# One dense batch instead of two, and block batches turned by TensorE, in a BigBird attention and SwiGLU kernel

## The chip, the cores and the metric

The kernel runs on one core of a Trainium2 chip. Its time is the device time of one execution in microseconds; three executions took 307.23, 308.00 and 308.08 us, median 308.0 us. A profile of one execution (307.95 us) records when every engine was busy and every DMA transfer ran. The engines are TensorE (PE: matmuls, with weight loads counted apart as PEld), VectorE (DVE), ScalarE (ACT), GpSimd (POOL) and SyncE (SP, which only issues DMAs here). Each engine works through its own list of instructions in a fixed order; an instruction that has to wait holds up all that stand behind it in that list. DMAs are issued from the lists of SP, ACT and POOL.

## What is computed

Four batches, eight heads, 768 tokens, head width 64. Attention is block-sparse: the 768 tokens are 24 blocks of 32, and a query block sees its neighbours, the first and last block, and three sampled blocks; the first and last query block see everything. After it comes a SwiGLU feed-forward layer (FFN) on 3072 tokens of width 512, with 1536 hidden columns.

```python
scores = scale * np.matmul(q, k.transpose(0, 1, 3, 2))
mask = np.abs(blk_i - blk_j) <= 1
mask = mask | (blk_i == 0) | (blk_j == 0) | (blk_i == n_blocks - 1) | (blk_j == n_blocks - 1)
for qb in range(n_blocks):
    for kb in sampled_blocks[qb]:
        mask[qb*32:(qb+1)*32, kb*32:(kb+1)*32] = True
attn = softmax(np.where(mask, scores, -1e9)); o = np.matmul(attn, v)
x = o.transpose(0, 2, 1, 3).reshape(B * S, H * D)
xn = x / rms(x) * rms_g
out = (silu(xn @ w_gate) * (xn @ w_val)) @ w_out
```

Inputs and outputs are float32; `sampled_blocks` holds int64. The kernel multiplies in bfloat16.

## The kernel before

**Tiles and units.** The 3072 tokens are 24 tiles of 128. Tiles are put into units (`UNITS`): a unit's tiles go through the FFN together, so a projection matmul (`proj`, line 728) moves 128 columns for each tile of the unit. Batch 0 has units of 1, 1, 1 and 3 tiles, each of the batches 1 to 3 two units of 3, which makes ten units, 0 to 9. For a unit `u` and a group `f` of hidden columns the steps are `g` (gate projection, PE), `th` (tanh, ACT), `uu` (DVE), `v` (value projection, PE), `hp` (DVE); then `y` (output projection, PE, line 767), `yo` (scaling, ACT or DVE) and `so` (store, SP).

**Dense batches** (`NDB = 2`: batches 0 and 1). All 768 x 768 scores of each head are computed. The mask is not added: the keys carry 24 more rows that say which block a key is in, and the queries 24 rows with 0 or -32768 for each block, so that the matmul of 88 rows (`dk`, line 322) gives masked scores. `de` is the exponential (ACT, line 343), `av` the product with the values (`dav`, line 357), `xo` the division by the sum (DVE). Batch 0's keys and queries are turned (head dimension onto the partitions) by TensorE transposes (`tpx`, line 301), batch 1's by DMA transposes on SP's queue (`turn`, line 288).

**Block batches** (`NDB` to 3: batches 2 and 3). Keys, queries and values are loaded (lines 452 and 459, SP), converted into bfloat16 rows (`fill_k`, `fill_q`, `fill_v`: `sfk`, `sfq`, `sfv`), and keys and queries are turned by one DMA transpose each for a batch (`turn_k`, line 478; `turn_q`, line 504). The two token halves `c` of a pair of tokens lie apart in the turned keys. For a tile `n` of four query blocks the keys that it sees are gathered into `kg`: `kf` copies neighbours and the first and last block (`kg_fixed`; DVE or ACT), `kd` the sampled blocks, at addresses from registers (`kg_sampled`, POOL, line 146). The values go back to DRAM as bfloat16 rows (`st`, `store_v`, line 508) and are gathered from there: `pvi` (`pair_v`, lines 570 to 578, SP) fixed blocks, `gv` and `gw` (`block_v`, line 555) sampled ones, one DMA of 32 rows for each, two thirds on SP and one third on ACT. `qk` (line 599) are the scores of a tile, `exp` (line 605), `av` (line 648), `xo`. Tile 5 (`AT`) holds the first and last block, which see all keys (`qka`, line 615; `expa`, line 623).

**Block numbers.** DVE works out the row and column addresses of the sampled blocks (`table`), and they are loaded into registers of POOL (three loads), SP (three) and ACT (two) (`table_regs`, line 435), 16 or fewer at a time.

**Units into the FFN.** `sq`, `rsq`, `xq` normalise a unit's attention output; for units below `NPET = 6` it is turned by TensorE (`tr`, line 704) and evicted (`cp`); for the later ones by a DMA transpose on SP's queue (`xt`, line 715).

**Order.** The kernel is scheduled by a planner that runs when the program is built: `op(key, engines with a cost, what it depends on, priority, function, slots it takes, slots it gives back)` registers a step, and a loop picks, over all steps that are ready, the one that can start first (then by priority) and emits its instructions. So the lists of all engines follow from costs and priorities written in the code, and the chip keeps to these lists. Attention steps have better priorities (1 to 3) than projections (4, 5). PSUM is eight banks: scores take two at a time from 0 to 3 (`S_`), gate projections bank 4 (at some times also 6), value projections 5, output projections 6, attention output 7. Buffers have slots (`pools`): two for gathered keys, three for gathered values, three for raw loads.

Of the kernel before, what the change touches and what calls it, by code (L numbers as in the profile page):

```python
# [16 lines left out]
def kernel(  # L17
# [19 lines left out]
    P = 128  # L37
# [12 lines left out]
    NR, NHP, NXN, NYO, NPET = NRND, 2, 2, 3, 6  # L50
    NSLOT, NAUG, NOPEN, NDB = 5, 2, 2, 2
    IXAT, RGAT = 36.0, 48.0
    NPT, NPA, NKG, NVG, NRAW = 4, 2, 2, 3, 3
    AHEAD, HURRY, HURU = 0.8, ("av", "xo", "sq", "rsq", "xq", "tr", "cp"), 0
    NSTARV, ZPAT, NG2 = 3, 32.0, 4
    AH = {"uu": 0.3, "hp": 0.3}
    WARM = (11, 10, 2)
    HD = NC * D // 2
    UNITS = [(0, 0, 1), (0, 1, 1), (0, 2, 1), (0, 3, 3)]
    UNITS += [(b, c, 3) for b in range(1, NDB) for c in (0, 3)]  # L60
    ND = len(UNITS)
    for b in range(NDB, B):
        UNITS += [(b, (5, 0, 1), 3), (b, (2, 3, 4), 3)]
    NU = len(UNITS)
    HG = [("h", 0 if u < 3 else u) for u in range(NU)]
    HO = [u if u < 3 else 0 for u in range(NU)]
# [9 lines left out]
    def bank16(n):  # L76
# [12 lines left out]
    VAC = const.tile([P, 2, H * NC, D + 2], BF16, name="VAC")  # L89
    VGC = const.tile([P, 6, VW], BF16, name="VGC")  # L90
# [6 lines left out]
    RAWD = list(A)  # L97
    RAWS = [RAWC[:, i * RB:(i + 1) * RB] for i in range(NRAW)]
    aug = [AUG[:, i] for i in range(NAUG)]
    va_ = [VAC[:, i] for i in range(2)]  # L100
    vfl = [t.rearrange("p m d -> p (m d)")[:, 0:6 * VW] for t in va_]
    VAUG = [t.rearrange("p (t c h d) -> p t c h d", t=NC // 2, c=2, h=H) for t in (vfl[0], PTC[:, 10240:10240 + 6 * VW])]
    rt_ = RAWC[:, NRAW * RB:].bitcast(BF16)
    VGB = [VGC, rt_[:, 0:6 * VW].rearrange("p (x w) -> p x w", w=VW),
           vfl[1].rearrange("p (x w) -> p x w", w=VW)]
    PD = [PTC[:, i * PDW:(i + 1) * PDW] for i in range(3)]
    PTB = [t.rearrange("p (h l x) -> p h l x", h=2, l=2) for t in [rt_[:, 6 * VW:6 * VW + 1024]] + [
        PTC[:, i * 1024:(i + 1) * 1024] for i in range(NPT - 1)]]
    PAB = [PTC[:, 3072 + i * 2048:3072 + (i + 1) * 2048].rearrange("p (l h x) -> p l h x", l=2, h=2) for i in range(NPA)]
    KTB = [t.rearrange("p (a s) -> p a s", a=NP) for t in (xs_[3], xs_[1])]  # L110
    QTB = [t.rearrange("p (a s) -> p a s", a=NP) for t in (xs_[4], PTC[:, 7168:7168 + NP * S])]
    KGB = [xs_[i].rearrange("p (x a s j c) -> p x a s j c", x=6, a=NP, s=4, j=16) for i in (0, 2)]
    KROW = AUG[:, 0].rearrange("p i e c x -> p (i e c x)").rearrange(
        "p (a c t x) -> p a c t x", a=NP, c=2, t=NC // 2)
    QROW = AUG[:, 1].rearrange("p i e c x -> p (i e c x)").rearrange("p (a n x) -> p a n x", a=NP, n=NC)
    kvv = [t.rearrange("b h (t p c) d -> b p (h t) (c d)", p=P, c=2) for t in (k, v)]
    qvv = q.rearrange("b h (n p) d -> b n p h d", p=P)
# [32 lines left out]
    zt = const.tile([P, VW], BF16, name="zt")  # L150
# [36 lines left out]
    nc.gpsimd.memset(zt[0:32, P:VW], 0.0)  # L187
# [9 lines left out]
    for t in va_:  # L197
        nc.vector.memset(t[:, :, D:D + 1], 1.0)
# [72 lines left out]
    def load(g, i):  # L271
        b, pr = divmod(g, NP)
        if i == 0:
            rawd[g] = RAWD[held["rawd", g][1]]
        nc.sync.dma_start(out=rawd[g][:, i], in_=(kv, qv, vv)[i][b, :, 2 * pr:2 * pr + 2, :])

    def fill(g, i, eng):
        copy(eng, aug[g % NAUG][:, i, :, :, 0:D],
             rawd[g][:, i].rearrange("p h (c d) -> p h c d", d=D))

    def pad_v(g, eng):
        b, pr = divmod(g, NP)
        src = rawd.pop(g) if b else A[g]
        copy(eng, va_[b][:, 2 * pr * NC:2 * (pr + 1) * NC, 0:D],
             src[:, 2].rearrange("p h (c d) -> p (h c) d", d=D))

    def turn(g):
        nc.sync.dma_start_transpose(
            out=X[g % NSLOT].rearrange("p i e (c t) -> p (i e c) t", t=P),
            in_=aug[g % NAUG].rearrange("p i e c r -> p (i e c r)"))  # L290

    def zero_pad(i):
        nc.vector.memset(aug[i][:, :, :, :, KQ:P], 0.0)
# [15 lines left out]
    held, rawd = {}, {}  # L309
# [38 lines left out]
    def dav(u, pr, bk):  # L348
        b, c0, nt = UNITS[u]
        pt, va = pts.pop((u, pr)), va_[b]  # L350
# [24 lines left out]
    tab_, at_ = VGB[0].rearrange("p x w -> p (x w)"), [0]  # L375

    def small(n, dt, p=P):
# [7 lines left out]
    kti, vti = small(NS * 2, I32, 1), small(NS * NR, I32, 1)  # L385
    koff, voff = {}, {}

    REGS = {"POOL": [("k", 0, 16), ("k", 16, 32), ("k", 32, 2 * NS)], "SP": [("v", 0, 16), ("v", 16, 32), ("v", 32, 2 * NS)],
            "ACT": [("v", 2 * NS, 2 * NS + 11), ("v", 2 * NS + 11, 3 * NS)]}
    HALF = 1024  # L390

    def load_table():
        nc.sync.dma_start(
            out=stab.rearrange("p n r i -> p (n r i)"), in_=s64.rearrange("n x -> (n x)").unsqueeze(0))
        for b in range(NDB, B):
            for lo in (0, S + 32):
                nc.sync.dma_start(out=vrows[b][lo:lo + 32, :], in_=zt[0:32, :])

    def table(i, eng):
# [3 lines left out]
        elif i == 1:  # L403
            TC(out=sf, in_=stab[:, 1:NB - 1, :, 0])
            TS(out=d2, in0=sf, scalar1=16.0, scalar2=None, op0=ALU.mult)
            TC(out=kti[:, 0:NS], in_=d2[:, :, 0])
            TS(out=d1[:, :, 0], in0=d2[:, :, 2], scalar1=float(HALF), scalar2=None, op0=ALU.mult)
# [24 lines left out]
    def table_regs(eng, part):  # L432
# [5 lines left out]
        for i_, x in enumerate(got_):  # L438
            r, n = divmod(lo + i_, NS)
            {"k": koff, "v": voff}[w][n * NR + r] = x  # L440
# [882 lines left out]
```

## Time and profile before

| quantity | value |
|---|---|
| median of three executions | 308.0 us |
| profiled execution | 307.95 us |
| its span, first to last instruction | 306.2 us |
| PE busy | 284.4 us, 93% of the span |
| DVE busy | 195.1 us, 64% |
| ACT busy | 175.2 us, 57% |
| POOL busy | 80.3 us, 26% |
| mean granted TensorE clock | 0.989 |
| DMA | 48.50 MB, 158 GB/s over the span |

The span is 1.75 us shorter than the execution. A matmul's end in the records is modelled and matmuls overlap, so PE's busy time is more than its work and a busy PE is not one at its peak; the spacing of equal matmuls that follow each other says what one costs. The chain of waits is followed back from the last instruction; printed in order of time, each piece is a start, a length, an engine or DMA and a line. In the table by stretches, each row has the stretch, its length, then for each engine its busy time and its instructions in it, the granted clock, the DMA engines' share and GB/s.

### The profile page before, as it was taken

The numbers are of one execution on the slowest core, as the hardware profiler recorded it, in microseconds if no ns is written. First come the engines' busy times: TensorE is split into PE (matmuls) and PEld (weight loads), VectorE is DVE, ScalarE is ACT, GpSimd is POOL, SyncE is SP. The second block draws the span as 40 slices with busy tenths as digits, with TensorE's granted clock in tenths as the row PEclk, the third lists the DMA queues.
The fourth block names the chain that finished last, engine by engine and source line by source line (L and its number), as shares of the span: only waits on it lengthen the run. The fifth ranks groups of instructions, "written<-read, shape, count | busy, mean of one in ns | idle before, by whom it ended". The sixth has DMA issues, their size and how long they took to land.

```text
span 306.2 us, 9818 instructions
## 1 busy us (share of the span) xinstructions
PE 284.4 (93%) x3838; PEld 183.4 (60%) x3838; DVE 195.1 (64%) x462; ACT 175.2 (57%) x290; POOL 80.3 (26%) x196
## 2 busy tenths in 40 slices
PE   8999989889999998999779699998699999999995
PEld 7899877666666664665445345564255655546543
DVE  6688896576756755877568435767177958807700
ACT  4899874468888785368554226877065424413322
POOL 4648100010024615119754200755041000100000
PEclk9999999999999999999999979999989999999999
DMA  7999999864799996783987973333754400060032
GB/s 218 364 242 157 203 268 323 182 229 80 119 267 266 182 308 161 159 239 87 263 196 187 195 157 97 90 84 89 166 127 135 92 36 2 0 156 0 1 98 109
DMA packets 85204, 48.50 MB, mean 158 GB/s; under 512 B 48037, under 2 KB 81318, under 8 KB 85158
## 3 DMA queue, kind: packets, MB, share of 16 engines
q1 hardware_dynamic: 76946, 41.63, 54.7%
q0 software_dynamic: 5792, 4.72, 10.1%
q10 hardware_dynamic: 2420, 1.53, 2.0%
q8 instruction: 30, 0.49, 0.6%
q14 instruction: 16, 0.13, 0.1%
HBM read 36.70 MB, written 8.02 MB: 146 GB/s over the span
## 4 chain that ended last, share of the span: by engine, by line
PE 67%; DMA 14%; DVE 8%; issue 5%; SPq 2%; ACT 2%; ACTq 1%; DVEq 0%
PE PS L728 33%; PE PS L767 15%; PE PS L322 7%; PE PS L357 4%; DMA RAWC<-in_v_dram 4%; PE PS L648 3%; DMA XC<-AUG 2%; DMA RAWC<-in_k_dram 2%; PE PS L301 2%; DMA VGC<-vrows 2%; DVE uu L743 2%; PE PS L599 2%; DMA xn<-xq 1%; DVE hp L754 1%; ACT th L737 1%
## 5 line engine op out<-in xcount | busy, mean ns | idle before, releaser
L737 ACT ACTIVATE th<-PS 128x384 bf16<-128x384 f32 x96 | 46.5, 492 | 81.9 <-PE PS L728 37.5
L743 DVE SCALAR_TENSOR_TENSOR uu<-th,PS 128x384 bf16<-128x384 bf16 x96 | 52.4, 551 | 49.4 <-ACT th L737 47.1
L728 PE MATMUL PS<-xn,wg 128*128 128x384 bf16 (+1 forms) x480 | 74.3, 294 | 7.3 <-DVE uu L743 4.2
L343 ACT ACTIVATE PTC<-PS 128x768 bf16<-128x768 f32 x92 | 70.4, 815 | 14.0 <-PE PS L322 13.8
L728 PE MATMUL PS<-xn,wv 128*128 128x384 bf16 (+1 forms) x480 | 77.9, 297 | 0.1
L767 PE MATMUL PS<-wo,hp 128*128 128x512 bf16 (+1 forms) x300 | 71.4, 376 | 4.1 <-DVE uu L743 4.1
L754 DVE TENSOR_TENSOR hp<-uu,PS 128x384 bf16<-128x384 bf16 x96 | 52.0, 551 | 16.8 <-PE PS L728 14.7
L728 PEld LDWEIGHTS <-wg 128*128 128x128 bf16 x480 | 40.7, 98 | 31.4 <-issue 9.0
L146 POOL COPY XC<-XC 128x128 bf16 x132 | 39.3, 371 | 62.6 <-PE PS L599 35.7
L728 PEld LDWEIGHTS <-wv 128*128 128x128 bf16 x480 | 40.5, 98 | 23.9 <-issue 1.9
L767 PEld LDWEIGHTS <-hp 128*128 128x128 bf16 x300 | 29.0, 99 | 32.4 <-issue 6.2
L322 PE MATMUL PS<-XC 88*128 88x128 bf16 (+1 forms) x288 | 42.6, 276 | 0.6 <-ACT PTC L343 0.6
L322 PEld LDWEIGHTS <-XC 88*128 88x128 bf16 x288 | 22.2, 100 | 7.8 <-issue 0.9
L357 PE MATMUL PS<-VAC,PTC 128*128 128x65 bf16 x552 | 21.1, 193 | 0.2 <-DVE XO L370 0.2
L357 PEld LDWEIGHTS <-PTC 128*128 128x128 bf16 x552 | 20.0, 97 | 2.0 <-issue 0.3
L777 ACT ACTIVATE yo<-PS 128x512 f32<-128x512 f32 (+1 forms) x16 | 9.1, 571 | 20.2 <-PE PS L767 20.1
L146 POOL CAST AUG<-RAWC 128x768 bf16<-128x768 f32 (+3 forms) x12 | 11.6, 973 | 30.1 <-DMA RAWC<-in_k_dram 25.7
L693 DVE SCALAR_TENSOR_TENSOR xq<-XO,rs,gB 128x512 bf16<-128x512 f32 x24 | 18.5, 792 | 0.2 <-POOL rs L686 0.2
L686 POOL TENSOR_TENSOR rs<-ms,nhalf 128x1 f32<-128x1 f32 (+1 forms) x6 | 4.3, 714 | 47.8 <-DVE ms L675 47.8
L605 ACT ACTIVATE PTC<-PS 128x1024 bf16<-128x1024 f32 x15 | 15.2, 1022 | 1.6 <-PE PS L599 1.1
L648 PEld LDWEIGHTS <-PTC 128*32 128x32 bf16 x736 | 8.1, 97 | 8.7 <-issue 7.4
L599 PEld LDWEIGHTS <-XC 64*128 64x128 bf16 x480 | 7.5, 93 | 6.9 <-issue 5.8
(112 smaller groups left out, 225.1 us busy)
## 6 DMA issues: line engine op xcount, KB each, us to landing
out_dram<-yo SPq DMA_DIRECT2D x21, 256.0 KB, 2.0
RAWC<-in_k_dram SPq DMA_DIRECT2D x4, 768.0 KB, 5.7
RAWC<-in_v_dram SPq DMA_DIRECT2D x4, 768.0 KB, 10.6
RAWC<-in_q_dram SPq DMA_DIRECT2D x12, 256.0 KB, 5.3
RAWC<-in_v_dram SPq DMA_DIRECT2D x7, 384.0 KB, 6.5
RAWC<-in_k_dram SPq DMA_DIRECT2D x6, 384.0 KB, 6.6
wg<-in_moe_w_gate_dram POOLq DMA_DIRECT2D x4, 384.0 KB, 6.9
wv<-in_moe_w_val_dram POOLq DMA_DIRECT2D x4, 384.0 KB, 7.9
```

The lines of the kernel that those rows point to most:

```text
L146: nc.gpsimd.tensor_copy(out=out, in_=in_)
L322: nc.tensor.matmul(out=s_[:, e, j * w:(j + 1) * w], lhsT=x[0:KQ, 0, e, jt * P:(jt + 1) * P], rhs=x[0:KQ, 1, e, c0 * P:c0 * P + w], start=T ...
L343: nc.scalar.activation(out=pts[u, pr][:, g * kt:(g + 1) * kt].rearrange("p j e w -> p e j w"), in_=s_[:, :, 0:kt * w].rearrange("p e (j w) ...
L357: nc.tensor.matmul(out=o_[:, t, e, :], lhsT=pt[:, jt, e, t * P:(t + 1) * P], rhs=va[:, (2 * pr + e) * NC + jt, 0:D + 1], start=(jt == 0), ...
L605: nc.scalar.activation(out=t_.rearrange("p h l x -> p (h l x)"), in_=tiles.pop(("s", b, n, pp)).rearrange("p h l x -> p (h l x)"), func=AF ...
L648: nc.tensor.matmul(out=o_[32 * i:32 * i + 32, a, :], lhsT=l_, rhs=r_, start=i not in begun, stop=k_ == last[i], tile_position=(0, 32 * i), ...
L693: nc.vector.scalar_tensor_tensor(out=xqs[u][:, t, :], in0=xos[u, t].rearrange("p h d -> p (h d)"), scalar=mss[u][:, t:t + 1], in1=gB, op0= ...
L728: nc.tensor.matmul(out=p_[:, j, :].rearrange("p (t w) -> p t w", w=P), lhsT=w_[:, c, f_ * P:(f_ + 1) * P], rhs=xns[u][:, :, c, :], start=( ...
L737: nc.scalar.activation(out=t_, in_=tiles["gp", u, f], func=AF.Tanh, scale=0.5)
L743: nc.vector.scalar_tensor_tensor(out=t_, in0=tiles.pop(("th", u, f)), scalar=1.0, in1=tiles.pop(("gp", u, f)), op0=ALU.add, op1=ALU.mult)
L754: nc.vector.tensor_tensor(out=hps[u][:, f * fg:(f + 1) * fg, :], in0=tiles.pop(("uu", u, f)), in1=tiles.pop(("vp", u, f)), op=ALU.mult)
L767: nc.tensor.matmul(out=tiles["yp", u, t, h], lhsT=hps[u][:, f, t * P:(t + 1) * P], rhs=wo[:, f, x], start=(f == 0), stop=(f == NF - 1))
```

## The change

Batch 1 becomes a block batch (`NDB = 1`), so there are three of them. Their tiles are put into units of 1, 2, 1, 2 tiles (batch 1), 1, 2, 3 (batch 2) and 3, 3 (batch 3): thirteen units in all. `NPET` is 7, so units 7 to 12 are turned by DMA.

Keys and queries of block batches are loaded with one token in a row of 64 numbers (256 bytes) and keep natural order. TensorE turns them: twelve 128 x 128 transposes into two PSUM banks (`ttk`, `ttq`, two of each for a batch), and one ACT copy of 128 x 1536 evicts them (`turnk`, `turnq`). Gathered keys need no halves any more, so `kf` (DVE alone now) and `kd` copy runs of 32 or more neighbouring elements. The keys of tile 5 are read with a stride of three, because values keep three tokens in a row (`NT3`).

The block numbers are packed in base 32, four to a register for `k` (three key blocks and a value block) and four query blocks to a register for the values. POOL loads 22 registers in two loads, ACT 6 in one, SP 6 in one; each use shifts and masks. The sampled values of a tile are issued in thirds: `r = 0` on SP, `r = 1` on ACT, `r = 2` on POOL. There are four slots for gathered values and five for exponentials. Raw loads of a batch come in the order values, keys, queries; batch 1's two key loads stand in SP's list behind the waits for the FFN weights (`gate_sync`), where batch 1's dense loads stood. The conversions of batch 1 are done by DVE or POOL, of batch 2 by POOL, of batch 3 by DVE, ACT or POOL.

```diff
-    NR, NHP, NXN, NYO, NPET = NRND, 2, 2, 3, 6
-    NSLOT, NAUG, NOPEN, NDB = 5, 2, 2, 2
-    NPT, NPA, NKG, NVG, NRAW = 4, 2, 2, 3, 3
-    AHEAD, HURRY, HURU = 0.8, ("av", "xo", "sq", "rsq", "xq", "tr", "cp"), 0
-    NSTARV, ZPAT, NG2 = 3, 32.0, 4
+    NR, NHP, NXN, NYO, NPET = NRND, 2, 2, 3, 7
+    NSLOT, NAUG, NOPEN, NDB = 5, 2, 2, 1
+    NPT, NKG, NVG, NRAW = 5, 2, 4, 3
+    AHEAD, HURRY, HURU = 0.4, ("av", "xo", "sq", "rsq", "xq", "tr", "cp"), 0
+    NSTARV, ZPAT, NG2 = 3, 32.0, 20
+    HD, NT3 = NC * D // 2, (1, 3, 1)
+    SPLIT = (((5,), (0,1), (2,),( 3, 4)), ((5,), (0, 1), (2, 3, 4)), ((5, 0, 1), (2, 3, 4)))
-    UNITS += [(b, c, 3) for b in range(1, NDB) for c in (0, 3)]
-        UNITS += [(b, (5, 0, 1), 3), (b, (2, 3, 4), 3)]
+        UNITS += [(b, ns, len(ns)) for ns in SPLIT[b - NDB]]
...
-    REGS = {"POOL": [("k", 0, 16), ("k", 16, 32), ("k", 32, 2 * NS)], "SP": [("v", 0, 16), ("v", 16, 32), ("v", 32, 2 * NS)],
-            "ACT": [("v", 2 * NS, 2 * NS + 11), ("v", 2 * NS + 11, 3 * NS)]}
+    REGS = {"POOL": [("k", 0, 16), ("k", 16, NS)], "DVE": [("k", 0, 16), ("k", 16, NS)],
+            "ACT": [("v", 0, NG4)], "SP": [("w", 0, NG4)]}
...
+    def field(x, i, top):
+        return nc.s_assert_within((x >> 5 * i if i else x) & 0x3E0, 0, 32 * top, skip_runtime_bounds_check_because=WHY)
...
-    def turn_k(b):
-        KTs[b] = KTB[held["KT", b][1]]
-        nc.sync.dma_start_transpose(
-            out=KTs[b].rearrange("p a (n x) -> p (a n) x", x=P), in_=KROW.rearrange("p a c t x -> p (a c t x)"))
+    def turn(b, x, j, bk):
+        t_ = PS[:, bk[0]:bk[0] + 2].rearrange("p b x -> p b x").bitcast(BF16)[:, :, 0:S].rearrange(
+            "p a (c w) -> p a c w", w=P)
+        tiles["turn", b, x, j] = t_
+        for a in range(2):
+            for c in range(NC):
+                nc.tensor.transpose(out=t_[:, a, c, :], in_=(KROW if x == "k" else QROW)[:, 2 * j + a, c, :], identity=ident)
+
+    def turned(b, x, j, eng):
+        ts, tb, n_ = (KTs, KTB, "KT") if x == "k" else (QTs, QTB, "QT")
+        ts[b] = tb[held[n_, b][1]]
+        copy(eng, ts[b][:, 2 * j:2 * j + 2, :], tiles.pop(("turn", b, x, j)).rearrange("p a c w -> p a (c w)"))
...
     def kg_sampled(b, n, xs, eng):
-        kg = new_kg(b, n).rearrange("p x a s j c -> p x a c s j")
-        kt = KTs[b].rearrange("p a (c y) -> p a c y", c=2)
+        kg = new_kg(b, n)
         for x, r in xs:
-            kb = k_at(blocks(n)[x] - 1, r)
-            copy(eng, kg[:, x, :, :, r, :], kt[:, :, :, bass.ds(kb, 16)])
+            copy(eng, kg[:, x, :, r, :], KTs[b][:, :, bass.ds(k_at(blocks(n)[x] - 1, r, eng), 32)])
...
-    def block_v(b, n, x, r):
-        (nc.scalar if r == 2 else nc.sync).dma_start(
-            out=new_vg(b, n)[32 * r:32 * r + 32, x, :],
-            in_=vrows[b][bass.ds(voff[(blocks(n)[x] - 1) * NR + r], 32), :])
+    def block_v(g, n, x, r):
+        (nc.sync, nc.scalar, nc.gpsimd)[r].dma_start(
+            out=new_vg(g, n)[32 * r:32 * r + 32, x, :],
+            in_=vrows[g][32:S + 64, :][bass.ds(v_at(blocks(n)[x] - 1, r), 32), :])
...
-                    lhsT=KTs[b][HS[h], pr, m * P:(m + 1) * P] if m < NC else kg[HS[h], min(m - NC + 2, 4) if m < NC + 2 else 5, pr],
+                    lhsT=KTs[b][HS[h], pr, m // NT3[1] * NT3[1] * P + m % NT3[1]:(m // NT3[1] + 1) * NT3[1] * P:NT3[1]] if m < NC else kg[HS[h], min(m - NC + 2, 4) if m < NC + 2 else 5, pr],
...
+        for x in "kq":
+            for j in range(2):
+                op(("tt" + x, b, j), {"PE": 12 * 0.056}, [("sf" + x, b, j, c) for c in range(2)], (TTP, b, j),
+                   lambda e, p, a=(b, x, j): turn(*a, p), [(S_, ("tt" + x, b, j))], [(x + "row", b)])
+                op(("turn" + x, b, j), pick_({"ACT": 1.45, "DVE": 1.75}, TTE), [("tt" + x, b, j)], (-0.5, b, j),
+                   lambda e, p, a=(b, x, j): turned(*a, e), [(x.upper() + "T", b)], [(None, ("tt" + x, b, j))])
```

## The prediction

> **What bounds the kernel now.** I read the page's first part, then the table of 10 us stretches, then the chain of waits in order of time, and last the rows of single lines for prices.
>
> The page:
>
> ```profile
> PE 284.4 (93%) x3838; PEld 183.4 (60%) x3838; DVE 195.1 (64%) x462; ACT 175.2 (57%) x290; POOL 80.3 (26%) x196
> ```
>
> PE is the bound on average. The stretches say where it is not (second number: PE's busy time in 10 us; behind the POOL figure: granted clock, DMA share):
>
> ```profile
> 100.00:110.00 10.00, 10.00 (x103) 6.31 (x100) 7.33 (x15) 8.24 (x12) 6.34 (x10) 1.00 1.20 229
> ...
> 150.00:160.00 10.00, 6.74 (x173) 4.11 (x171) 5.87 (x15) 5.28 (x12) 4.48 (x15) 1.00 0.87 235
> ...
> 170.00:180.00 10.00, 6.97 (x31) 3.21 (x29) 3.62 (x7) 2.23 (x6) 1.54 (x6) 0.84 1.05 216
> ...
> 210.00:220.00 10.00, 5.94 (x29) 2.69 (x28) 3.94 (x8) 2.35 (x4) 2.83 (x10) 1.00 0.57 138
> ```
>
> From 70 to 120 us (batch 1 dense, beside the FFN) no stretch has idle PE. From 120 to 240 us (block batches 2 and 3) the twelve rows leave 13.7 us idle, and two rows have a clock of 0.84 and 0.83, worth 3.3 us more. Idle elsewhere: 1.9 us up to 20, 3.0 from 30 to 70, 3.2 behind the last matmul. From 240 to 300 PE is full with FFN alone.
>
> The chain shows causes, and the prices of matmuls (start, length, what):
>
> ```profile
> 12.76 1.15 PE PS L322 x18
> ...
> 26.22 0.67 PE PS L728 x12
> ...
> 70.03 0.75 PE PS L704 x12
> ...
> 71.43 1.14 PE PS L357 x36
> 72.57 0.65 PE PS L322 x4
> ...
> 98.49 0.65 PE PS L767 x3
> ...
> 153.53 0.64 PE PS L648 x59
> 154.17 0.68 PE PS L599 x44
> ...
> 167.34 6.75 DMA XC<-AUG
> ...
> 195.54 0.61 PE PS L615 x36
> ...
> 215.88 4.16 DMA xn<-xq
> ```
>
> The DMA transpose of batch 3's keys (167.34) ends the chain into the 170 to 180 stretch; the transpose of unit 7's input (215.88) does so at 220. Single lines:
>
> ```profile
> L435 ACTq TENSOR_LOAD <-VGC x2: 4107/4732/5358, 50.1 to 56.7; - x2
> L555 ACTq DMA_DIRECT2D RAWC<-vrows x12: 322/323/1342, 117.6 to 223.7; - x12
> L248 POOL DMA_DIRECT2D wg<-in_moe_w_gate_dram x4: 788/806/1149, 13.3 to 27.6; - x4
> 225.26 3.49 POOL L146 COPY XC<-XC 128x128 bf16 x12 [12.43 <-PE PS L599]
> ```
>
> (min/median/max in ns; the last is a run of twelve sampled-key copies, 0.29 us each; another run, from 208.47, took 4.35, 0.36 each.)
>
> **PE's work, before.** A 384-column matmul is 0.65/4 = 0.163 us, a 128-column one 0.67/12 = 0.056 in a projection and 1.15/18 = 0.064 in a score, a 65-column one 1.14/36 = 0.032, a 512-column one 0.65/3 = 0.217, a transpose 0.75/12 = 0.0625, the small block ones 0.0155 (line 599), 0.017 (615) and 0.013 (648: 0.64/59 to, at 205.88, 0.83/64). With the counts: FFN 672 x 0.163 + 288 x 0.056 + 276 x 0.217 + 24 x 0.108 = 188; dense attention 144 x 0.163 + 144 x 0.064 + 576 x 0.032 = 51; block attention 480 x 0.0155 + 144 x 0.017 + 896 x 0.013 = 21.5; transposes and warm-up some 12. Together 272.5 of 306.2: some 33.7 us are lost, of which the stretches place 25.1 (13.7 + 3.3 + 1.9 + 3.0 + 3.2); the remaining 8.6 I can't place, since ends of matmuls are modelled.
>
> **What the change does to PE's work.** Out: batch 1's 96 wide scores (15.6) and 288 value products (9.2), -24.8. In: one more block batch, 240 x 0.0155 + 72 x 0.017 + 448 x 0.013 = +10.8; turning three batches, 144 x 0.0625 = +9.0. Units turned by TensorE hold 10 tiles instead of 12, -0.5. Projections: 384 matmuls of 384 columns, 288 of 256 (0.108) and 576 of 128, 125.8 us instead of 125.6, +0.2. Sum -5.3 us. The keys of tile 5 read with stride three (144 weight loads) no row shows; between nothing and a doubling of 0.017 that is 0 to +2.4, and I take 0, since weight loads run beside the matmul before.
>
> **What it does to the lost time.**
> 1. No DMA transposes of keys and queries. SP was busy issuing eight of them (17.9 + 8.2 + 8.1 = 34 us by the rows of lines 288, 478, 504), and ACT's gather DMAs of 169 to 175 us stood behind one. The stretch 170 to 180 lost 3.0 idle and 1.6 of clock: -4.6. Next late there would be the evictions ( of 1.44 us on ACT by the unit copies of 128 x 1536, four a batch, 17 in all). ACT has room: 48 dense exponentials of 0.815 (39) and its gathered-key copies (11.5) go, 14 exponentials of 1.02 (14.3), the evictions and 22 more gather issues at 0.32 (7) come.
> 2. Register loads. The two on ACT (4.1 and 5.4 us) stand before tanh in the chain; the stretches 50 to 70 lose 1.7 us. One load of 6 registers stays: between 0 and -1.7, I take -1.2.
> 3. The other block-stage losses, 17.0 - 4.6 = 12.4 us in two batches, are 6.2 a batch. A third batch adds between 0 (it runs beside as much FFN as before) and +6.2; a fourth value slot and SP without transposes let gathers start earlier, so I take +3.
> 4. The FFN's own DMA transposes stay and are six instead of four; the dearest one cost 4.2 us of chain, others nothing in the stretches. Counted within point 3.
> 5. POOL gets 66 gather DMAs. Each costs between ACT's issue (0.32) and a weight load's (1.15), 21 to 76 us in all, in front of key copies. Its work for a block batch: 66 copies (19 to 24), 22 gathers (7 to 25), conversions up to 12 x 0.83 (10), norms 3 x 1.1: 39 to 62, while PE has six tiles of FFN (47) plus attention and turning (13.6), 61 us. So it fits beside PE, just: taken at 0, upper end in the rivals.
> 6. Loads of keys and queries in 256-byte rows: batch 2's query loads are 256-byte rows too and landed in 5.3 us, against 5.7 for keys three times as large; DMA has room (share under 0.6 from 180 on). 0. Base-32 packing: about ten DVE instructions of 0.2 us on one partition, once, beside PE at 40 to 56 us; 0.
>
> Sum: -5.3 - 4.6 - 1.2 + 3 = -8.1. Span 306.2 - 8.1 = 298.1; with the 1.75 around it 299.9, so **300 us** in place of 307.95, 2.6% less. The profiled execution lies at the median (308.0).
>
> One rule speaks against point 5. Row first: weight DMAs issued by POOL took 0.74 to 1.15 us each, beside DVE copies. The Trainium skill, SBUF — State Buffer, on the trap that DVE blocks DMA, says that GpSimd can't write descriptors while a DVE copy holds the port that they share, so a DMA of 620 ns alone takes about 3100 ns. An estimate by that page: at 3.1 us the 66 gathers would be 205 us and POOL would set the end far above 308; at 620 ns they would be 41 us and hidden. No run here shows a small DMA from POOL beside such copies.
>
> **Rivals.**
> - *POOL sets the pace (slower).* For: 198 copies and 66 gathers in one list, and a gather that waits for a free value slot holds all key copies behind it. Against: POOL is at 26% now. Beginning when registers are there (about 60 us), POOL needs 3 x (24 + 10 + 3.3) = 112 us plus gathers; behind the last copy there remain the last unit's attention (some 4) and FFN (23.4). The end passes 308 when 60 + 112 + 66g + 27 > 306, so at g = 1.6 us a gather (1.1 if POOL also waits 10 us a batch). At 1.8: 60 + 112 + 119 + 27 = 318.
> - *Batch 1 comes late (about the same).* Before, 48 us passed from the first block-key load (84.7) to the first block scores (132.9), hidden under dense batch 1. Now that chain starts at the weight gate (36 us) and half of it waits for raw slots. Cover: batch 0's attention ends near 59.8, then 31 us of its FFN remain, to 91. 36 + 48 = 84 fits; if slots add 15, PE waits 8 us: 308.
> - *Block-stage losses mostly vanish (faster still).* If half of the 12.4 goes with SP's transposes and no third share comes: 300 - 3 - 6.2 = 291.
>
> **Chances.** Forecast as it stands (294 to 306) 0.50; losses vanish (291) 0.15; batch 1 late (303 to 313) 0.18; POOL sets the pace (from 310) 0.17. A measurement here tells 0.3% (0.9 us) from no change. Faster: 0.48 + 0.15 + 0.07; same: 0.02 + 0.03; slower: 0.17 + 0.08. The range runs from 288 (the case below the forecast, less 3) to 316 (batch 1 late with the stride's 2.4, and the lower part of POOL's case).
>
> **What would show it.** Right: 24 exponentials of 128 x 768 for batch 0's last unit instead of 72; no DMA transpose but six of xn; no idle PE behind a key transpose; PE's idle from 60 to 240 us about 17 us; POOL gathers under 1.1 us. Wrong: key copies of POOL that end PE's waits; PE idle at 75 to 95 us before the first ttq or qka; a row of low clock there.

## The result, and the profile after

The changed kernel takes 329.7 us (median of four, 326.5 to 330.2) beside 308.0 for the kernel before: a ratio of 1.068 (95% interval 1.061 to 1.076), 21 us more. The forecast was 300, and the range ended at 316. Below, a ratio is turned into microseconds by 308.0; the difference of two ratios is uncertain by some 3 to 4 us, which follows from their intervals. Some executions of one and the same kernel show a lower clock and take over 1.5% longer; ratios are of the others.

The page of the changed kernel, first part (busy time, share of the span, instructions; the span is 328.3 us):

```profile
PE 286.2 (87%) x4603; PEld 203.1 (62%) x4632; DVE 206.2 (63%) x500; ACT 159.6 (49%) x240; POOL 132.9 (40%) x345
```

PE's idle time is 328.3 - 286.2 = 42.1 us, where it was 21.8. No other engine is near its limit; POOL went from 26% to 40%. The table by stretches of the changed kernel says where (columns as in the prediction: PE's busy time is the second number, the granted clock stands behind POOL):

```profile
70.00:80.00 10.00, 4.35 (x33) 2.60 (x31) 9.91 (x16) 3.83 (x5) 9.70 (x28) 0.94 0.49 120
...
90.00:100.00 10.00, 5.60 (x186) 4.36 (x179) 3.58 (x10) 1.79 (x4) 4.76 (x10) 0.83 0.96 196
100.00:110.00 10.00, 9.89 (x207) 6.35 (x206) 8.45 (x22) 6.28 (x8) 8.09 (x25) 1.00 0.43 106
110.00:120.00 10.00, 6.06 (x176) 5.06 (x161) 4.01 (x13) 3.55 (x7) 2.40 (x8) 0.83 1.19 213
...
140.00:150.00 10.00, 8.95 (x56) 6.31 (x58) 5.25 (x11) 5.81 (x9) 6.83 (x19) 0.66 0.82 181
150.00:160.00 10.00, 8.80 (x189) 7.46 (x188) 5.22 (x11) 7.35 (x11) 6.33 (x13) 1.00 1.20 268
160.00:170.00 10.00, 7.83 (x224) 6.17 (x224) 4.33 (x13) 3.09 (x6) 5.29 (x14) 0.66 0.87 181
170.00:180.00 10.00, 8.97 (x245) 5.46 (x240) 6.53 (x15) 7.07 (x10) 8.42 (x28) 1.00 0.36 81
```

From 60 to 130 us, where the kernel before lost 2.2 us under dense batch 1, PE is idle for 14.4; from 130 to 260 for 18.4 (before: 12.4). Low clock, summed as busy time times (1 - clock) over all stretches, went from 3.2 to 10.8 us. So idle time gives +20.3 and the clock +7.6, and the span grew by 22.1: by this estimate PE's work itself shrank by some 5.8 us.

The chain of waits of the changed kernel, in order of time (start, length, what):

```profile
22.68 11.88 DMA wg<-in_moe_w_gate_dram
...
70.65 7.26 DVE XC L152 x9
...
84.71 5.43 DMA RAWC<-in_v_dram
...
92.20 4.27 DMA VXC<-vrows
...
112.61 3.93 issue
...
155.55 6.46 DMA PTC<-vrows
...
180.44 3.35 DMA xn<-xq
```

There is no single culprit to be seen. A weight load (22.68), nine neighbour-key copies in a row (70.65), a value load (84.71), gathers (`vrows`, 92.20 and 155.55) and the FFN's input transpose (180.44) each hold up the chain at some point. PE's waits by cause (us in all, times, longest) read the same way:

```profile
PE PS L696 <- DVE uu L711: 6.3, 4, 3.5
PE PS L616 <- DMA VXC<-vrows: 4.4, 2, 4.0
PE PS L696 <- issue: 3.9, 1, 3.9
PE PS L616 <- DMA PTC<-vrows: 2.8, 3, 1.4
PE PS L696 <- DMA xn<-xq: 2.8, 2, 2.4
PE PS L583 <- POOL XC L150: 2.8, 1, 2.8
PE PS L696 <- DMA wg<-in_moe_w_gate_dram: 2.5, 2, 1.7
PE PS L471 <- POOL AUG L150: 2.1, 1, 2.1
```

PE's direct waits for gathered values are 7.2 us of 42. Read alone, this table says that gathers are a minor cause. The runs say otherwise.

Single lines of the changed kernel: first sampled gathers on ACT, POOL and SP (duration of the issuing instruction, min/median/max in ns), then ACT's register load, then POOL's sampled-key copies (busy us, mean ns):

```profile
L523 ACTq DMA_DIRECT2D PTC<-vrows x34: 322/322/1204, 64.0 to 243.9; - x34
L523 POOL DMA_DIRECT2D VXC<-vrows x32: 496/496/801, 66.2 to 243.4; - x32
L523 SPq DMA_DIRECT2D VXC<-vrows x32: 315/324/2104, 91.5 to 238.0; - x32
```

```profile
L429 ACTq TENSOR_LOAD <-VXC x1: 3513/3513/3513, 58.6 to 58.6; - x1
```

```profile
L150 POOL COPY XC<-XC 128x128 bf16 x198 | 51.1, 303 | 10.0 <-PE PS L567 6.9 <-PE PS L583 2.7 <-POOL XC L150 0.2
```

### The profile page after: what moved, and what is told of

Its sections match the earlier page's. It is cut to its first block, busy times and chain, and to the rows that moved or that the text cites. A ratio compares the mean times of both kernels' runs of the same rounds, so it can differ in the third digit from the quotient of the medians.

```text
span 328.3 us, 12386 instructions
## 1 busy us (share of the span) xinstructions
PE 286.2 (87%) x4603; PEld 203.1 (62%) x4632; DVE 206.2 (63%) x500; ACT 159.6 (49%) x240; POOL 132.9 (40%) x345
## 3 DMA queue, kind: packets, MB, share of 16 engines
q0 software_dynamic: 7904, 6.92, 12.4%
## 4 chain that ended last, share of the span: by engine, by line
PE 61%; DMA 16%; DVE 8%; issue 8%; SPq 3%; POOL 2%; POOLq 1%; ACT 1%; ACTq 0%
PE PS L696 29%; PE PS L735 15%; PE PS L616 5%; DMA RAWC<-in_v_dram 4%; DMA wg<-in_moe_w_gate_dram 4%; DMA PTC<-vrows 3%; PE PS L567 3%; DVE XC L152 3%; DMA VXC<-vrows 3%; PE PS L305 3%; DMA xn<-xq 2%; PE PS L340 2%; PE PS L471 2%; PE PS L284 1%; SPq L523 1%
## 5 line engine op out<-in xcount | busy, mean ns | idle before, releaser
L696 PE MATMUL PS<-xn,wg 128*128 128x128 bf16 (+2 forms) x624 | 76.6, 271 | 11.7 <-DVE uu L711 6.3
L705 ACT ACTIVATE th<-PS 128x384 bf16<-128x384 f32 (+1 forms) x90 | 45.9, 512 | 82.4 <-PE PS L696 68.1
L696 PE MATMUL PS<-xn,wv 128*128 128x128 bf16 (+2 forms) x624 | 80.1, 275 | 4.6 <-issue 3.9
L711 DVE SCALAR_TENSOR_TENSOR uu<-th,PS 128x384 bf16<-128x384 bf16 (+1 forms) x90 | 51.9, 579 | 45.7 <-ACT th L705 43.7
L696 PEld LDWEIGHTS <-wg 128*128 128x128 bf16 x624 | 50.6, 100 | 29.8 <-issue 11.0
L722 DVE TENSOR_TENSOR hp<-uu,PS 128x384 bf16<-128x384 bf16 (+1 forms) x90 | 50.9, 577 | 23.9 <-PE PS L696 23.2
L696 PEld LDWEIGHTS <-wv 128*128 128x128 bf16 x624 | 51.0, 102 | 23.9 <-issue 6.5
L150 POOL COPY XC<-XC 128x128 bf16 x198 | 51.1, 303 | 10.0 <-PE PS L567 6.9
L326 ACT ACTIVATE PTC<-PS 128x768 bf16<-128x768 f32 x44 | 33.3, 815 | 5.8 <-PE PS L305 5.7
L747 DVE TENSOR_SCALAR yo<-PS 128x512 f32<-128x512 f32 (+1 forms) x19 | 12.4, 661 | 16.4 <-PE PS L735 14.3
L305 PE MATMUL PS<-XC 88*128 88x128 bf16 (+1 forms) x192 | 21.4, 248 | 0.9 <-ACT PTC L326 0.8
L152 DVE COPY XC<-XC 128x256 bf16<-128x256 bf16 (+1 forms) x63 | 21.1, 383 | 0.7 <-PE PS L567 0.7
L652 POOL TENSOR_SCALAR rs<-ms 128x1 f32<-128x1 f32 (+2 forms) x9 | 3.3, 362 | 43.8 <-ACT sc L640 34.4
L523 POOL DMA_DIRECT2D VXC<-vrows x32 | 16.6, 518 | 9.9 <-issue 5.0
L150 POOL CAST AUG<-RAWC 128x768 bf16<-128x768 f32 (+2 forms) x19 | 14.8, 791 | 13.9 <-DMA RAWC<-in_k_dram 10.8
L523 POOL DMA_DIRECT2D PTC<-vrows x34 | 17.2, 506 | 6.2 <-issue 5.2
L616 PEld LDWEIGHTS <-PTC 128*32 128x32 bf16 x1056 | 12.9, 101 | 10.8 <-issue 8.9
## 6 DMA issues: line engine op xcount, KB each, us to landing
RAWC<-in_k_dram SPq DMA_DIRECT2D x6, 768.0 KB, 10.1
```

The source lines that it names most:

```text
L150: nc.gpsimd.tensor_copy(out=out, in_=in_)
L152: nc.vector.tensor_copy(out=out, in_=in_)
L305: nc.tensor.matmul(out=s_[:, e, j * w:(j + 1) * w], lhsT=x[0:KQ, 0, e, jt * P:(jt + 1) * P], rhs=x[0:KQ, 1, e, c0 * P:c0 * P + w], start=T ...
L326: nc.scalar.activation(out=pts[u, pr][:, g * kt:(g + 1) * kt].rearrange("p j e w -> p e j w"), in_=s_[:, :, 0:kt * w].rearrange("p e (j w) ...
L523: (nc.sync, nc.scalar, nc.gpsimd)[r].dma_start(out=new_vg(g, n)[32 * r:32 * r + 32, x, :], in_=vrows[g][32:S + 64, :][bass.ds(v_at(blocks( ...
L616: nc.tensor.matmul(out=o_[32 * i:32 * i + 32, a, :], lhsT=l_, rhs=r_, start=i not in begun, stop=k_ == last[i], tile_position=(0, 32 * i), ...
```

## The experiments

The first theory was that the block form of batch 1 is what costs, since its chain of steps has no dense matmuls beside it. Rivals: the parts common to all block batches (turning, gathers on three queues, small units); the clock; single waits.

**Batch 1's attention left out, in both kernels.** The steps of batch 1 are not emitted and cost the planner nothing; a DVE copy fills the units' input.

```diff
+        if skipped(key):
+            engs, fn, d = {e_: 0.001 for e_ in list(engs)[:1]}, SK.get(key), 0.0
```

> The changed kernel with batch 1's attention left out (its loads, conversions, turning, gathers, scores and products; a copy of a constant into the units' input stands in for it, the FFN of batch 1 stays). Three block-batch theories: (own) the block form of batch 1 is itself what costs: PE work 10.8 + 3 of turning, 14 us of PE idle between 70 and 115 us and some 4 us of low clock go, so 329.7 - 32 = about 298. (Rival: the parts common to all block batches, turning by TensorE, gathers on POOL, the new order, cost as much in batches 2 and 3): only the PE work of batch 1 goes, about 316.

> The kernel before with batch 1's dense attention left out in the same way (loads, conversions, turning, scores, exponentials, products; a copy of a constant stands in). Dense batch 1 is 24.8 us of PE work, so 308 - 25 = 283 if the block batches 2 and 3 don't need its cover, up to 291 if they do. Own theory: the changed kernel without batch 1's attention stands within 8 us of this one (it has 6 us more PE work for turning two batches and the same block batches otherwise). Rival (common parts): it stands 20 us or more above.

Measured: 294.3 us (ratio 0.956, 0.952 to 0.961) and 288.3 (0.935, 0.929 to 0.941). Block batch 1 costs 1.068 - 0.956 = 34.4 us, dense batch 1 cost 20.0. So 14.4 of the 21 us lie in the swap, and 6.6 in batches 2 and 3, whose form changed only in its details. The two kernels without batch 1 are 6.0 us apart, inside the 8 that the first theory gave. Both sides hold a part; the swap holds the larger.

**The clock.** Idle matmuls into free banks, in five places where PE waits.

```diff
+    FILL = {("ttq", 1, 0): 34, ("av", 4, 0, 0): 64, ("qka", 2, 0): 44, ("g", 10, 0): 38}
+        if k_ in FILL:
+            idle(FILL[k_], bk[0])
+        if k_ == ("ttq", 1, 1):
+            idle(56, 7)
```

> The changed kernel with 236 idle matmuls of 128 columns (about 13 us of PE work) put in five of the places where PE waits (before the first query turning, the projection behind it, the first value product of batch 1, the first scores of batch 2, the first projection of unit 10). If the low granted clock (0.66 to 0.94 in nine of the stretches from 70 to 190, worth some 13 us) follows from PE's gaps: mean clock from 0.958 to 0.975 or more and the time down by 5 to 10, to 320 to 325. If the clock falls for another reason: clock as it was, time 330 to 335.

Measured: 327.4 us, ratio 1.062 (1.055 to 1.069), clock 0.963: between the two expectations. Three stretches of this run:

```profile
70.00:80.00 10.00, 9.28 (x117) 7.38 (x115) 6.77 (x18) 6.08 (x7) 9.92 (x28) 1.00 0.58 144
80.00:90.00 10.00, 10.00 (x163) 6.47 (x161) 5.28 (x11) 6.38 (x10) 3.21 (x8) 1.00 0.95 253
90.00:100.00 10.00, 10.00 (x243) 7.70 (x244) 5.65 (x14) 2.57 (x4) 5.16 (x12) 1.00 0.72 148
```

Where PE was kept busy the clock stayed at 1.00 (0.94, 0.89 and 0.83 without the fillers), so here the low clock follows PE's gaps. But later stretches were low instead (the sum is still 10.2 us), and the total isn't told apart from the changed kernel's. This run alone leaves open whether the clock is a cause of its own; the run without gathers, below, has neither the gaps nor any low clock.

**Turning by TensorE alone**, in the kernel before, which has this way as an option:

```diff
-    PEQ, PEK = (), ()
+    PEQ, PEK = (2, 3), (2, 3)
```

> The kernel before, with block batches' keys and queries turned by TensorE (six transposes for a pair of heads into one bank, evictions on DVE or ACT) in place of DMA transposes; nothing else. By the prediction's terms: PE work +6, the loss behind the key transpose -4.6, so about 309.5. Rival (turning by TensorE is what costs): 314 or more. Rival (turning is the gain that another part hides): 304 or less.

Measured: ratio 1.008 (1.004 to 1.013), some 2.6 us more, as the two terms have it in sum. In the profile, idle time fell by 1.5 us and low clock by 1.0 while the span grew by 2.6, so it is rather +5 of PE work and -2.5 of waiting than +6 and -4.6. Turning, in this form, isn't what costs 21.

**Order.** 3 us are added to when the planner thinks that the inputs of PE's block-attention steps are there, in both kernels.

```diff
-                t0 = max(t0, end[d])
+                t0 = max(t0, end[d] + (3.0 if late(o["key"]) else 0.0))
```

> The changed kernel, with the planner told that the inputs of PE's block-attention steps (ttk, ttq, qk, qka, av) come 3 us later than its costs say; so projections that are ready are put ahead of these steps in PE's list, and the costs of all steps stay. Seen in the trace of the changed kernel: its block scores start later and later against the order that they were given (4 us at 60, 9 at 82, 16 at 99, 22 at 128, 40 at 201). Theory (the work to cover batch 1's chain is there, but stands behind the waits in PE's list): PE's gaps of over 0.6 us sum to 18 or less in place of 31, the clock rises, 312 to 320 us. Rival (there is no such work left at 70 to 115 us): gaps of the same sum elsewhere, 326 to 332.

> The kernel before with the same 3 us for qk, qka and the block batches' av. Its block scores start late by 5 us at 133 to 22 at 236. If its 13.7 us of idle PE from 120 to 240 are waits with ready projections behind them, 6 to 8 go: 300 to 302. Rival (the key transposes and late gathers leave nothing to put there, or the FFN so moved lacks at the end): 307 to 310.

Measured: ratios 1.062 (1.053 to 1.072) and 1.007 (1.003 to 1.011). PE's idle time in the changed kernel is 40.6 us after 42.1. So idle time moved and did not go: PE then waited for the inputs of other steps (3.2 us up to 113 before a unit's turning, 4.4 up to 181 for an `xn`). The first run (323.8 us) lies between its two expectations, the second (307.7) inside the range of its rival.

**Single waits.** The waits for weights moved ahead of the value loads; POOL's gathers moved to ACT (with a register load of their block numbers there); tiles in units of three, as before the change (with NPET 6).

```diff
-                gate = 2 + hf if b == NDB and i == 0 else None
+                gate = 2 + hf if b == NDB and i == 1 else None
```
```diff
-        (nc.sync, nc.scalar, nc.gpsimd)[r].dma_start(
+        (nc.sync, nc.scalar, nc.scalar)[r].dma_start(
```
```diff
-    SPLIT = (((5,), (0,1), (2,),( 3, 4)), ((5,), (0, 1), (2, 3, 4)), ((5, 0, 1), (2, 3, 4)))
+    SPLIT = (((5, 0, 1), (2, 3, 4)),) * 3
```

> The changed kernel with the waits for the second and third FFN weights put before batch 1's two value loads in SP's list, in place of its two key loads; so no block load runs beside the first weights. If the early value loads delay the weights: the two waits for weights at 27 and 33 us (2.5 us) go, weights land in 7 us in place of 12, 325 to 327. Rival (batch 1 is the later for it, since its values go through DRAM): the wait before its first value product (4.0 us at 92) grows by as much or more, 330 to 336.

> The changed kernel with the 66 sampled-value gathers of POOL issued by ACT instead (a second register load of 6 numbers there); POOL does copies and conversions alone. If POOL's list (0.72 us a gather, 47 us in all, in front of its copies) sets the lateness: the waits on POOL copies (2.1 us at 70, 2.8 at 138) and on values gathered by POOL (3 us at 159 to 162) go, 318 to 325. Rival (the third issuing engine is what keeps gathers short; on ACT they stand between exponentials and tanh): 332 to 340.

> The changed kernel with the tiles of all three block batches in two units of three (5, 0, 1 and 2, 3, 4), as before the change, and NPET 6; so 10 units in place of 13, and 48 projection pairs for batches 1 and 2 of 384 columns. If the small units cost (first projections of 128 and 256 columns, more steps on ACT and DVE, six more tanh): 322 to 327. If they help (the FFN of a first tile can start before the rest of its batch's attention): 333 to 340.

Measured: 1.059 (1.051 to 1.067), 1.074 (1.066 to 1.083) and 1.060 (1.049 to 1.072). The waits for weights at 27 and 33 us went with the first, but its first value product then waited 7.8 us in place of 4.0. All three stay far above 1: none of them is the cause by itself. Against the changed kernel they are not clear of noise (the third ratio rests on two executions), and no expectation held: the first came out 2 us under the lower range, the other two between their ranges.

**Five such edits together** (the weight wait, and the ones below, with 2 us of margin):

```diff
-    KFE, SQE, YOE = ("DVE",), ("DVE", "ACT"), ("DVE", "ACT")
-    TTE, TTP = ("ACT",), -1
+    KFE, SQE, YOE = ("DVE", "ACT"), ("DVE", "ACT"), ("DVE", "ACT")
+    TTE, TTP = ("ACT", "DVE"), -1
-    CE = {1: (DP_, DP_, DP_), 2: (P_, P_, P_), 3: (DAP_,DAP_,DAP_)}
+    CE = {1: (DP_, DP_, DP_), 2: (DAP_, DAP_, DAP_), 3: (DAP_,DAP_,DAP_)}
```

> The changed kernel with five edits that each aim at one of the waits seen: weight waits ahead of the value loads, neighbour-key copies on DVE or ACT, evictions of turned keys on ACT or DVE, batch 2's conversions on any of three engines, and 2 us of margin for PE's block-attention steps. If the loss is a set of separate waits: their shares add, some -12, 312 to 318. If a batch's whole way (loads, conversion, turning, copies, scores, gathers) is too long for the work that is left beside it, waits move instead of going: 320 to 327.

Measured: 317.3 us, ratio 1.034 (1.026 to 1.043). That is inside the range given to separate waits (312 to 318). Half of the loss came back, by 35.2 us of idle PE in place of 42.1 and 6.7 of low clock in place of 10.8. It is the fastest version here that does all the work, and still slower than the kernel before.

**Values or keys?** In batches 2 and 3, the emission of gathers (`gv`, `gw`, `pvi`) or of sampled-key copies (`kd`) is left out; all else keeps its order. The first of the two edits:

```diff
-        if o["fn"] is not None:
+        if o["fn"] is not None and not (k_[0] in ("gv", "gw", "pvi") and k_[1] > 1):
```

> The changed kernel with the value gathers of batches 2 and 3 left out (sampled and neighbour blocks, on SP, ACT and POOL; the products read what stands in the slots); all other instructions in the same order. If the gathers are what makes these two batches late: PE's waits on gathered values from 150 us on (0.7 + 1.4 + 0.7 + 0.7 at 159 to 171, 1.0 at 206) go, POOL and ACT are freed of 44 issues each (32 and 14 us), the clock of 140 to 190 rises, 318 to 322. If the keys' way or the FFN's input sets the pace there: waits move, 325 to 329.

> The changed kernel with POOL's sampled-key copies of batches 2 and 3 left out (132 copies of 0.29 us, 38 us; the scores read what stands in the slots); all other instructions in the same order. If POOL's list sets the lateness of batches 2 and 3 (its gathers stand behind these copies): waits on copies (2.8 at 138, 1.6 at 218) and on gathers go, 316 to 322. If not: only 1 to 3 us go, 325 to 329.

Measured: 310.8 us (1.016, 1.007 to 1.025) without the gathers, more than the 8 to 12 us that were expected to go; without the 132 key copies 326.0 and 326.5 beside 306.4 for the kernel before, a ratio of 1.065. Taking 38 us of work off POOL gave nothing that can be told from noise; taking the gathers away gave 16 us (1.068 - 1.016), 8 a batch, and PE's idle time from 130 to 260 us fell from 18.4 to 5.7. From 60 to 130 us, under batch 1, it stayed at 14.9.

**All gathers left out, in both kernels.** The value products read the batch's own rows in SBUF, as many and as large; the gathers are not emitted, as above.

```diff
-                w += [(i, p1[:, 32 * i:32 * i + 32], vg[:, i, hd]) for i in range(4)]
+                w += [(i, p1[:, 32 * i:32 * i + 32], vaugs[b][:, i, 4 * pp + a, :]) for i in range(4)]
```

> The changed kernel with all value gathers of the three block batches left out (the products read the batch's own value rows that stand in SBUF, equally many and equally large; the rows are still stored); all other instructions in the same order. Without those of batches 2 and 3 it was 310.8. If a gathered batch costs 9 to 10 us: some 300 to 303. If batch 1's gathers matter less, since its wait for the stored rows stays hidden: 306 to 310.

> The kernel before with all value gathers of its two block batches left out in the same way. If a gathered batch costs the same 9 to 10 us there, the third one accounts for 9 to 10 of the 20 lost: 286 to 289. If the gathers are mostly hidden in the kernel before (dense batch 1 and fewer issuing queues), and the changed one made them dear: 298 to 304.

Measured: 293.3 us (0.954, 0.949 to 0.959) and 295.0 (0.958, 0.952 to 0.965). Without gathers the changed kernel is as fast as the one before. The gathers cost it 35.1 us; they cost the kernel before 12.9, 6.4 a batch. The first run is faster than both its ranges, the second lies between its two. The three batches don't pay alike: with those of batches 2 and 3 gone, the gathers of batch 1 still cost 1.016 - 0.954, 19 us. Stretches of the changed kernel without gathers:

```profile
90.00:100.00 10.00, 8.81 (x198) 5.70 (x199) 7.54 (x21) 5.34 (x8) 8.15 (x27) 1.00 1.21 226
...
110.00:120.00 10.00, 9.79 (x166) 7.45 (x161) 5.11 (x12) 8.69 (x12) 7.92 (x22) 1.00 0.98 253
...
140.00:150.00 10.00, 8.91 (x265) 6.17 (x252) 7.06 (x19) 6.12 (x10) 7.16 (x18) 1.00 0.13 30
...
160.00:170.00 10.00, 9.89 (x138) 7.88 (x139) 6.74 (x13) 4.30 (x7) 0.12 (x1) 1.00 0.07 27
```

The gap at 90, the one at 110 and the low clock of 140 to 170 are gone (idle PE from 60 to 130 us is 3.3), and with them all but 1 us of the waits on `uu`, `xn` and `AUG` that had seemed to be causes of their own: idle PE 18.5 us, low clock 0. Both kernels without gathers are not told apart (1.3 us), although PE's work shrank by some 5: the changed one still has 18.5 us of idle PE where the one before has 14.6.

**Gathers issued, but read by nobody.** Same products as in the last run; every gather stays.

> The changed kernel with all gathers issued and moved as they are, but read by nobody (the products read the batch's own rows, as in the run without gathers); so PE waits for no landing and no gather waits for a slot that PE still reads. If those waits are the cost: within 5 us of the run without gathers (300 to 308). If the issues in the lists of SP, ACT and POOL, their wait for the stored rows, and the transfers are the cost: 318 to 329.

Measured: ratio 1.069 (1.061 to 1.077), the same as the changed kernel. PE waits for no gathered value any more, and just as long for other things, above all for POOL's conversions of loaded keys and queries:

```profile
PE PS L471 <- POOL AUG L150: 9.2, 6, 4.4
PE PS L695 <- DVE uu L710: 4.0, 3, 1.8
PE PS L695 <- DMA xn<-xq: 3.2, 1, 3.2
```

So neither PE's wait for a gather's landing nor a slot that PE still reads is what costs. What is left is what a gather does to other steps: the wait for the store of the batch's rows, the issues in the lists of SP, ACT and POOL, and the bytes.

**Three runs that take these apart**, all with gathers that nobody reads, and with plain copies in place of the six `xn` transposes. The run that they are compared with (1.069) still has the transposes. First, gathers, sampled and fixed, from a tensor that is filled once, early:

```diff
-            in_=vrows[g][32:S + 64, :][bass.ds(v_at(blocks(n)[x] - 1, r), 32), :])
+            in_=vfix[32:S + 64, :][bass.ds(v_at(blocks(n)[x] - 1, r), 32), :])
```

> As the run whose gathers nobody reads (327.7), but every gather reads a DRAM tensor that one transfer of 1 MB fills once, at some 60 us, instead of its batch's stored rows; so no gather waits for a batch's store. All issues, address instructions and gather transfers stay. The FFN's input transposes of units 7 to 12 are plain copies on the same queue (in both runs here). If the lists are held by the wait for the store: 295 to 305. If the issues and transfers cost: 316 to 328.

Second, without the gathers of ACT and POOL:

```diff
-        if o["fn"] is not None:
+        if o["fn"] is not None and not (k_[0] == "gw"):
```

> As the run whose gathers nobody reads (327.7), with the 66 sampled-value gathers on ACT and the 66 on POOL left out; SP's 66 and its neighbour blocks stay, and wait for the stored rows as they did. The FFN's input transposes of units 7 to 12 are plain copies on the same queue. If gathers in the lists of ACT (in front of exponentials and tanh) and POOL (in front of conversions and copies) are the cost: 295 to 304. If those in SP's list (in front of loads and of the FFN's input) or the transfers are: 312 to 326.

Third, with 16 bytes of each row, in fixed gathers too:

```diff
-            out=new_vg(g, n)[32 * r:32 * r + 32, x, :],
+            out=new_vg(g, n)[32 * r:32 * r + 32, x, 0:8],
```

> As the run whose gathers nobody reads (327.7), but each row of a gather is 16 bytes in place of 1040 (fixed blocks too), so 13 MB fewer are moved; issues, address instructions, rows and waits for the stored rows stay. The FFN's input transposes of units 7 to 12 are plain copies on the same queue. If the bytes of the gathers are what costs, beside the loads: 295 to 310. If the issues (and the rows' descriptors) in the lists of SP, ACT and POOL are: 318 to 331.

Measured: 1.078 (1.067 to 1.088), 1.018 (1.009 to 1.027) and 1.019 (1.011 to 1.027). Taking the wait for the store away, with plain copies, made nothing faster, so neither of the two explains what the other runs gain. Taken away in this order, the gathers of ACT and POOL cost 1.069 - 1.018, about 16 us, and SP's, sampled and fixed, the other 20 (1.018 - 0.954); this lies between the expectations of the second run. Without their bytes the gathers still cost 1.019 - 0.954 = 20 us, and the bytes 15. Neither expectation of the third run held: it is both, about half and half. PE's busy time and share in that third run, of a span of 313.4 us:

```profile
PE 278.9 (89%) x4603; PEld 197.1 (63%) x4632; DVE 206.7 (66%) x500; ACT 159.3 (51%) x240; POOL 134.9 (43%) x345
```

Its idle time, 34.5 us, lies between the 42.6 of the run whose gathers nobody reads and the 18.5 without gathers.

**How a gather makes other steps late, as the traces show it.** SP's list in the changed kernel has batch 2's first value load at 84.71, behind fixed gathers that begin at 71.35, and the second half of its keys at 108.28, behind more gathers of batch 1:

```profile
84.71 0.45 SPq L449 DMA_DIRECT2D RAWC<-in_v_dram  x1
...
96.18 6.02 SPq L523 DMA_DIRECT2D PTC<-vrows  x8
102.54 2.41 SPq L523 DMA_DIRECT2D VXC<-vrows  x4
105.00 1.86 SPq L538 DMA_DIRECT2D VXC<-vrows  x2
...
108.28 0.47 SPq L449 DMA_DIRECT2D RAWC<-in_k_dram  x1
```

The same two loads without gathers:

```profile
71.45 1.16 SPq L449 DMA_DIRECT2D RAWC<-in_v_dram  x2
...
86.25 0.41 SPq L449 DMA_DIRECT2D RAWC<-in_k_dram  x1
```

So with gathers these loads go out 13 and 22 us later. In the run whose gathers nobody reads, the chain of waits runs through that key load, its conversion on POOL and the turning on PE, and PE stands idle for 4.4 us before the turning begins:

```profile
110.70 9.01 DMA RAWC<-in_k_dram
119.77 0.83 POOL AUG L150
...
122.56 0.82 PE PS L471 x6
```

Loads hold up gathers too. SP's 223 DMAs share eight semaphores in turn, and most of them wait until the DMA that had the same semaphore before has landed. In the run whose gathers nobody reads, a sampled gather is issued at 102.06 us, when a key load that was issued at 94.20 has landed (102.04), though it reads no keys. Of the 223, 141 are gathers. No run changed the number of semaphores, so what this sharing costs is not shown.

## Why the prediction was wrong, point by point

- *PE's work, -5.3.* Right, as far as the estimate from span, idle time and clock goes: -5.8.
- *1, no key and query transposes, -4.6 (with +9.0 of turning in PE's work).* Right in kind, too large: turning alone moved the kernel before by +2.6, where the terms gave +1.4, and by its profile waiting fell by 2.5 us, not 4.6. (The 1.6 us of clock in the term were taken over all of the 10 us; over PE's 6.97 busy ones they are 1.1.)
- *2, register loads, -1.2.* Fits: the stretches 50 to 70 hold 0.65 us of idle PE in place of 1.7. ACT's load took 3.5 us, not 4.1 and 5.4.
- *3, the third block batch's losses, 0 to +6.2, taken as +3: this step failed first.* It divided the lost time of the two old block batches by two and took the result, 6.2 us, as the most that a third one could add. For the old batches the size was about right: leaving their gathers out gave 6.4 a batch. It didn't carry over to the new one: batch 1's gathers cost 19 us in the changed kernel, those of batches 2 and 3 together 16 in place of 12.9. That is 22 us more, which is the whole loss.
- *5, 66 POOL gathers, 0: this step failed with it.* The price of one was inside the bounds (0.50 us, 0.72 from one to the next). The error was to compare POOL's sum of work with PE's sum. The gathers cost although no engine is full: 198 sampled and 75 fixed ones stand in three in-order lists, among conversions, exponentials, tanh, loads and stores that PE needs soon. With gaps of up to 0.4 us counted in, the runs of sampled gathers and their address instructions take 44.5 us of ACT's list (27.1 before) and 49.5 of SP's (51.1), and POOL's some 47 are new. That this list time, with 15 us for the bytes, is how they cost is what the last runs leave over; the traces show it for single places, as above, and not as a sum.
- *4, six `xn` transposes.* Not priced by themselves. One ended a wait of 2.4 us at 181, as one did before; without gathers none did.
- *6, 256-byte rows, 0.* Left open: key loads took 10.1 us to land, query loads of 768 KB 9.1 (before: 5.7, and 5.3 for query loads of 256 KB); without gathers they took 7.1 and 8.0, and with POOL's gathers on ACT 5.4 and 8.1 at no gain in time. Longer rows weren't tried.

The rivals. *POOL sets the pace* ended on the right side for the wrong reason: its condition, 1.1 to 1.6 us a gather, was not met, and neither 38 us less work on POOL nor its gathers on ACT made the kernel faster. *Batch 1 comes late* named the right place: the rows of 70 to 120 us, idle and with low clock, as written under "wrong". It gave 8 us of waiting; there are 14.4, and the clock on top. Of the 66 POOL gathers nine ran beside a DVE copy or cast (`L152`) and took 496 to 801 ns; the others took 496 to 593. The Trainium skill, SBUF — State Buffer, in "A bandwidth-pool intuition that's wrong", has about 3100 ns for a DMA of 620 beside a DVE copy; a delay of that size wasn't seen. The forecast's range missed because no case let gathers on SP and ACT cost anything beyond their old share.

What stays open is why the gathers of batch 1 cost 19 us where those of a later batch cost 8, and 6.4 in the kernel before. The missing dense batch is one candidate: the kernel before was idle for only 2.2 us from 60 to 130, under dense batch 1, and 14.4 of the 21 us lie in the swap. But the third queue, the order of loads and the units changed with it; moving POOL's gathers back to ACT alone changed nothing. Dense batch 1 next to gathers of three queues wasn't tried.

## What to carry to other kernels

Price small DMAs by leaving them out, not by the waits that name them: here they ended 7 of 42 us of PE's waits, and without them the whole loss was gone, since other steps had come late through them. And a price read where other work covers it needn't hold for one more of the same: 6.4 us a batch became 19 for the new one. Before dense work is exchanged for cheaper work with a longer chain, ask what the dense work had been covering, which no sum of engine work tells. When one wait after another is removed and the total stays, look for what all the late steps share.

## What was unexpected in the hardware

- The granted clock fell to 0.66 in two stretches (140 to 150, 160 to 170), each with waits of only 2.8 us in all around its start (one up to 140.8; three close together up to 162.0), and came back to 1.00 in the stretches between. Where gaps were filled (70 to 100) it stayed at 1.00, and in the run without gathers throughout.
- At 112.6 us PE stood for 3.9 us before a projection while nothing that the profile shows held it. The same line (`PE PS L696 <- issue: 3.9, 1, 3.9`) stands in the waits of two runs with the same order of instructions, one without the value gathers of batches 2 and 3, one without the key copies.

- Cutting the bytes of the gathers, with all issues kept, was worth 15 us, though the table gives the DMA engines a share of 0.43 and 0.36 in stretches like 100 to 110 and 170 to 180 us (1.19 and 1.20 in 110 to 120 and 150 to 160).
